# A windowed attention and gated-expert kernel: one written instruction order from the first tile's output stage on, for the DMA queue too, and the second batch's roots in folded form

## The chip, the cores and the metric

The program runs on one core of one Trainium2 chip. A core has five engines with queues of their own: TensorE (PE in the profile; its weight loads are PEld), VectorE (DVE), ScalarE (ACT), GpSimd (POOL) and SyncE (SP), which here issues nearly all DMAs. Each engine takes its own instructions strictly in the order of the program and waits on semaphores for the others. The metric is the device time of one execution in microseconds; the time of a kernel is the median of its runs.

## The reference

Inputs: `q`, `k`, `v` of shape (8 batches, 8 heads, 576 positions, 64), and the weights of a gated expert.

```python
scores = scale * (q @ k.T)                      # per batch and head
mask = (rel >= 0) & (rel < 64)                  # causal window of 64 positions
attn = softmax(where(mask, scores, -1e9))
x = (attn @ v) -> (4608 tokens, 512)            # heads side by side
rms = sqrt(mean(x * x, -1) + 1e-6)
xn = x / rms * rms_g
g, val = xn @ w_gate, xn @ w_val                # 512 -> 1536
out = (g * sigmoid(g) * val) @ w_out            # 1536 -> 512, float32
```

## The kernel before, in words

**Tiling.** Attention runs batch by batch and, in a batch, by pairs of heads: 4 pairs a batch, 32 in all, numbered n = 0 to 31. A batch has 576 tokens; the expert works on 9 tiles of 512 tokens, so tile 1 takes its first 64 tokens from batch 0 and the rest from batch 1, and tile 2 starts with the last 128 tokens of batch 1. Values and weights of the expert are kept as a high and a low half-precision part, and each product is three matmuls (`three`, lines 960 to 962). In tile t the stage *in* (`expert_in`, blocks c = 0 to 5, each two columns groups of gate `pg` and value `pv`) makes the gated activation `h`, and the stage *out* (`expert_out`) sums 6 blocks for each of 4 token groups into `po`, which ACT scales into `ot` and SP stores (L1232). From tile 3 on (`FIRST7`) the in stage uses a seven-product form (`expert_in_7`, `product`, L1136) with combined weights.

**Start.** Batch 0 is done at the start. Meanwhile the weights, which arrive as 8-byte numbers, are loaded into staging buffers (`stage`, L202: three buffers of tag `st8`), widened on ACT, PE and DVE (`widen_powers` L215/L216, `widen_rest` L224 to L227) and split into high and low parts (`split`, L238 to L246). `w_out` is scaled by one common power of two, whose small steps (L306 to L321, with the matmul `obound`) come ahead of its split.

**Combined weights.** `prepare(c, step)` makes the seven combinations of block c of the weights and puts them into a scratch tensor in memory, `sevens`: at step 0 twelve copies of plain blocks (L1091), at others sums on DVE (`sums`, L1061, L1096 to L1109), a high part on ACT (L1083), a low part on DVE (L1073) and two stores (L1075). `load_sevens` (L1119) loads them back into `wt` for tile 3 and later. `PREP` spreads these steps: nine over slots 58.5 to 72, the rest over slots 78 to 192.

**Pairs from batch 2 on** (n >= 8). At `visit(n)` PE makes the products of pair n (`sc`, L399) and the weighted values of pair n-2 (`xp`, L534). Then, a fraction of a slot apart, come masks on DVE (L412), exponentials on ACT (L415), 16 moves on POOL (`pm`, L381) and three transposes on DVE (L386, L388), due ahead of visit n+2. The key load of pair n (`load_kv`, L346 to L360; three buffers) is written 7 steps ahead of visit n; its buffer is that of pair n-3, last used by the sum of squares (L614) behind visit n-1.

**What sets the order.** Work is written into the program at *steps* (32 a tile: 24 for the in stage, 8 for the out stage) or *slots* (48 for an in stage of tiles 0 to 2, 42 later, and 24 for an out stage; one slot of the out stage is one call of `chunk_out`, six matmuls). `at_step` and `at_slot` put a part into `plan`, and `tick` writes what is due between matmul groups. What is written is then placed by the framework's planner, which orders each engine's instructions by its own model of their times, so that an instruction can run ahead of others that were written earlier. `in_written_order(start, engines)` takes that freedom away: from instruction `start` on, each instruction of the listed engines is chained to the one written before it on the same engine, without a semaphore. `strict["on"]` goes with it: while it is on, `defer` writes a copy and a subtraction of the activation one or two ticks later (L1028, L1029) instead of at once.

In the kernel before, `ORDERED = (1, 1)`: the written order starts with block 1 of tile 1, for PE, DVE, ACT and POOL; SP stays with the planner throughout.

**The roots.** After attention each batch needs 1/rms for each of its tokens. For batches 0 and 1 (`b < NRB`) `inverse_roots` sums the squares with five matmul groups (`tot`, L756), which put 128 tokens on partitions and five columns side by side; eleven small DVE steps on 128 x 5 (L774, L811) give the inverse root, and `broadcast` (L835) turns it into a row for all partitions. `normalise` then scales `xb` (L865) and makes both parts of `xn` (L869, L871). The events of batch 1 are due at steps 23.5, 24.5 and 27. For later batches `normalise_all` does the same with the *folded* roots: four matmuls sum the squares with 32 equal columns each (`tot`, L796), so that 144 tokens lie along the free axis and the four quarters of the batch on the four groups of 32 partitions; the eleven steps run on 128 x 144, in three parts; `spread` (L818) makes the row, and `scaled` (L900) and `part` (L910 to L913 for tiles below 3) do the rest. The parts are written a fraction of a slot apart.

Of the kernel before, what the change touches and what calls it, by code (L numbers as in the profile page):

```python
# [42 lines left out]
VISITS = (24.5, 29.5, 35, 41, 47.5)  # L43
MOVES = (8.7, 7, 4.5, 4)
FIRST7 = 3
ORDERED = (1, 1)
PREP = ((27.5, 32, 9), (35, 88, 41))
MASK_AT, MASK_BY, WEIGH = 1, 1, 1
MOVE_AT, MOVE_BY, TURN_AT = 11.3, 0.8, -4
NORM_AT, NORM_BY, NORM_GAP = 5, 0.75, 2  # L50
RUSH = 12
GATE, HH_7, HH_8 = 0, 1, 1
ST = 2 * NBLK * P - D
NRB = 2
S1, LK1, LV1, LQ1 = [-2, 1, 3, 6, 10, 12.5, 15, 18], 2.5, 5, 7
LN2_16 = 16 * math.log(2.0)
MASKED = -3.0e38
# [5 lines left out]
def tile_window_attention_moe(  # L63
# [10 lines left out]
    nc = tc.nc  # L74
# [13 lines left out]
    def in_written_order(start, engines):  # L88

        last = {}  # L90
        for k, ins in enumerate(nc.cur_bb.bb.instructions):
            if ins.engine not in engines:
                continue
            if k >= start and ins.engine in last:
                tc.add_manual_dep(ins, last[ins.engine].name, NO_SYNC, reason="written order")
            last[ins.engine] = ins
# [38 lines left out]
    for rows, cols, own in (  # L135
# [7 lines left out]
        part = mask[rows, cols]  # L143
# [287 lines left out]
    def scores_of_pair(n, sc, first):  # L431
# [19 lines left out]
        whole[n] = p, m, st[:, 2, :]  # L451
        by = MASK_BY if n >= RUSH else 0.5
        for i, u in enumerate(order):
# [177 lines left out]
    def attention_events(b, start, pace, tags):  # L631

        load_queries, load_keys, score, to_keys, values, roots, normal, moved, turned, products, drain, norm = attention(b)
        lk, lv, lq, n0, n1 = tags
        events = []
        if b < NRB:
            events = [(n0 - 1, roots), (n0, partial(normal, 0)), (n1, partial(normal, 1))]
        else:
            s0 = slot_at(visit_at(NPAIR * b + 5))
            for k, part in enumerate(normalise_all(b, norm)):  # L640
                at_slot(s0 + NORM_AT + NORM_BY * k + (NORM_GAP if k > 2 else 0), part)
        for hp in range(NPAIR):
            if b >= TB:
                n = NPAIR * b + hp
                i0 = visit_at(n) - half_steps * (b - 1)
                events.append((i0 - 7, partial(load_queries, hp)))
                events.append((i0 - 7, partial(load_keys, hp)))
                s0 = slot_at(visit_at(n))
                for k in range(16):
                    when = MOVE_AT + MOVE_BY * k if n >= RUSH else MOVE_AT - 4.7 + 0.5 * k  # L650
                    at_slot(s0 + when, partial(moved, hp, k // 4, k % 4))
                for k in range(3):
                    at_slot(slot_at(visit_at(n + 2)) + TURN_AT - 2 * (RUSH <= n < 16) + k, partial(turned, hp, k))
                visits[n] = partial(products, hp), partial(values, hp), partial(drain, hp)
                continue
            i0 = start[2 * hp]
            events.append((i0 - lq, partial(load_queries, hp)))
            events.append((i0 - lq, partial(load_keys, hp)))
            for g in range(2):
                i = start[2 * hp + g]  # L660
                events.append((i + lv, partial(values, hp, g)))
                events.append((i + lk, partial(to_keys, hp, g)))
                events.append((i, partial(score, hp, g)))
        return events
# [4 lines left out]
    def slot_at(h):  # L669

        t, r = divmod(h, half_steps)
        per = 4 * NF if t < FIRST7 else 7 * NC
        first = t * (4 * NF + NC * TT // P) - max(0, t - FIRST7) * (4 * NF - 7 * NC)
        return first + (r * per / in_phase if r < in_phase else per + (r - in_phase) * NC / 2)

    def step_at(s):

        t = 0
        while slot_at(half_steps * (t + 1)) <= s:
            t += 1  # L680
        s -= slot_at(half_steps * t)
        per = 4 * NF if t < FIRST7 else 7 * NC
        return half_steps * t + (s * in_phase / per if s < per else in_phase + (s - per) * 2 / NC)

    def at_slot(s, part):
        at_step(step_at(s) + 1e-6, part)
# [7 lines left out]
    def visit_at(n):  # L694

        n -= NPAIR * TB
        return VISITS[n] if n < 4 else VISITS[4] + 8 * (n - 4)
# [175 lines left out]
    def normalise_all(b, norm):  # L873
        return LazyParts(b, norm).parts()
# [93 lines left out]
    strict = {"on": False}  # L968
# [35 lines left out]
    def expert_in(t, c):  # L1004
        xn = xn_tiles[t]
        hs[t, c] = h_tile(t, c)
        for i in range(2):
            f = 2 * c + i
            fs = slice(i * P, (i + 1) * P)
            hh, hl = hs[t, c][:, 0, i, :], hs[t, c][:, 1, i, :]  # L1010
            acc = []
            for w, name in ((wg, "g"), (wv, "v")):
                tick(0.5)
                a = ps_mo.tile([P, TT], F32, tag="mo", name=f"p{name}_{t}_{f}")
                for kt in range(NKD):
                    if kt == 2:
                        tick(0.5)
                    if True:
                        three(a, w[c][:, 0, kt, fs], w[c][:, 1, kt, fs], xn[:, 0, kt, :], xn[:, 1, kt, :],
                              kt == 0, kt == NKD - 1)  # L1020
                acc.append(a)
                if name == "g":
                    th = wk.tile([P, TT], F32, tag="t2k", name=f"th_{t}_{f}", bufs=T2K)
                    nc.scalar.activation(th, a, AF.Tanh, scale=th_scale[:, c : c + 1])
                    nc.vector.scalar_tensor_tensor(th, th, 1.0, a, ALU.add, ALU.mult)
            nc.vector.scalar_tensor_tensor(th, acc[1], 2.0**-41, th, ALU.mult, ALU.mult)  # L1026
            hi_copy = nc.vector.tensor_copy if t < 2 and E('HHE', 'a' * 24)[12 * t + f] == 'v' else nc.scalar.copy
            defer(HH_8, partial(hi_copy, hh, th))  # L1028
            defer(HH_8 + 1, partial((nc.vector if t and c == NC - 1 else nc.gpsimd).tensor_tensor, hl, th, hh, ALU.subtract))  # L1029
# [204 lines left out]
    def expert_out(t):  # L1234
        for k in range(TT // P):
            halves = 2 if t == NT - 1 and k == TT // P - 1 else 1
            for e in range(halves):
                es = slice(e * DM // halves, (e + 1) * DM // halves)
                po = (ps_mo.tile([P, DM], F32, tag="mo", name=f"po_{t}_{k}_{e}") if t < FIRST7 else banks[(0, 2, 5, 1)[(k + e) % 4]])[:, es]
                for c in range(NC):  # L1240
                    if e == 0:
                        tick(Fraction(2, NC))
                    if t >= FIRST7 and c == k == 0:
                        continue
                    chunk_out(po, t, c, k, c == 0, c == NC - 1, es)
                store(po, t, k, es)
# [17 lines left out]
    def at_step(h, part):  # L1264
        plan.append((h, len(plan), part))
# [3 lines left out]
    for h, part in attention_events(1, S1, 0, (LK1, LV1, LQ1, 24.5, 27)):  # L1269
        at_step(h, part)  # L1270
# [49 lines left out]
    for a, z, count in PREP:  # L1320
        s0, s1 = slot_at(a), slot_at(z)
# [13 lines left out]
    rest(1)  # L1335
    first_full = 1
    for e in SEQ:
        if e[0] == "o":
            expert_out(int(e[1]))
        else:  # L1340
            expert_in(int(e[0]), int(e[1]))
        if e != "o0" and e != "O0" and e[0] != "0":
            first_full = 2
    for t in range(first_full, NTR):
        if t == FIRST7:
            early.close()
            ps_7 = ctx.enter_context(tc.tile_pool(name="ps_7", bufs=1, space=PSUM))
            banks.update((i, ps_7.tile([P, TT], F32, name=f"bk{i}")) for i in (0, 1, 2, 5))
            late = ctx.enter_context(tc.tile_pool(name="late", bufs=1))
            snaps.update((i, late.tile([P, TT], F32, name=i)) for i in ("s1", "u2"))  # L1350
        if t >= FIRST7:
            expert_in_7(t)
        else:
            for c in range(NC):
                strict["on"] |= (t, c) >= ORDERED
                if (t, c) == ORDERED:
                    written = len(nc.cur_bb.bb.instructions)
                expert_in(t, c)
                if t == FIRST7 - 1 and c % 2:
                    load_sevens(c // 2)  # L1360
        expert_out(t)
    assert not plan
    in_written_order(written, [e.engine for e in (nc.tensor, nc.vector, nc.scalar, nc.gpsimd)])
    early.close()


# [35 lines left out]
```

## Time and profile before

| | |
|---|---|
| median of 3 runs | 1026.49 us (1024.73 to 1028.15) |
| profiled execution, its own time | 1029.22 us |
| its span, first to last instruction | 1027.4 us |
| mean granted TensorE clock | 0.981 |
| busy: PE / DVE / ACT / POOL | 971.2 / 646.3 / 508.0 / 508.8 us |
| first output-stage matmul (L960, `po`) | 185.4 us |
| first matmul of tile 1 (`pg`) | 229.6 us |
| copies of plain weight blocks (L1091) | 72, issued from 49.3 to 166.7 us |

How to read it: times are microseconds from the first instruction. A row of the timeline gives start, duration, engine, line, operation, output<-input, and the number of merged instructions (x); in brackets stands the idle time before it and what ended that. In a row of the waits stand the waiter, what it waited for, the sum in us, the number of waits and the longest. A matmul lasts 0.38 us from start to end, but the next one starts 0.22 us after it (0.43 at half clock). SPq rows are issues of DMAs by SP's queue.

### The profile page before, as it was taken

What the parts mean: (1) busy time and instruction counts of PE and PEld (TensorE: products, weight loads), DVE (VectorE), ACT (ScalarE), POOL (GpSimd) and SP (SyncE); (2) the same over time, 40 slices, a digit from 0 to 9 for tenths busy, and PEclk for the clock granted to TensorE, in tenths of its full rate; (3) what the DMA queues carried; (4) which work ended last, traced back from release to release, by engine and by line L of the source; (5) the groups of instructions that cost most, each with busy time, mean ns of one, the idle gap of its engine ahead of it and who ended that gap; (6) DMA issues with size and microseconds to landing.
All of it is one profiled execution on the core that took longest, in us unless ns stands there. A gap on an engine that the chain in (4) does not pass through costs nothing.

```text
span 1027.4 us, 20830 instructions
## 1 busy us (share of the span) xinstructions
PE 971.2 (95%) x7835; PEld 630.7 (61%) x7835; DVE 646.3 (63%) x1721; ACT 508.0 (49%) x1303; POOL 508.8 (50%) x634
## 2 busy tenths in 40 slices
PE   7788979799999999999999999999999999999998
PEld 5544435344544544478747874787478848856875
DVE  5687846744789676656775677666766655522540
ACT  5557767424544545356545654565355524422540
POOL 3334624753976478637773776377647611200210
PEclk9989989799999999999999999999999999999999
DMA  7646683122332555256725672566245515632401
GB/s 281 193 139 202 197 267 78 58 72 68 90 103 66 150 165 169 67 163 197 223 66 170 201 223 67 158 212 211 66 143 170 175 32 159 196 108 92 145 1 41
DMA packets 81316, 143.43 MB, mean 140 GB/s; under 512 B 25792, under 2 KB 38336, under 8 KB 81216
## 3 DMA queue, kind: packets, MB, share of 16 engines
q1 hardware_dynamic: 80640, 140.93, 45.1%
q8 instruction: 61, 1.00, 0.4%
q10 hardware_dynamic: 576, 1.18, 0.3%
q14 instruction: 39, 0.32, 0.1%
HBM read 121.64 MB, written 20.45 MB: 138 GB/s over the span
## 4 chain that ended last, share of the span: by engine, by line
PE 68%; DVE 17%; ACT 7%; issue 3%; DMA 2%; POOL 2%; SPq 0%; DVEq 0%; ACTq 0%; POOLq 0%
PE bk L1136 18%; PE bk L960 5%; PE bk L961 5%; PE bk L962 5%; PE xp L534 4%; PE sc L399 4%; DVE th L1176 3%; ACT th L1167 3%; PE po L962 3%; PE po L961 3%; PE po L960 3%; DVE th L1177 3%; PE pg L962 3%; PE pg L960 3%; PE pv L960 3%
## 5 line engine op out<-in xcount | busy, mean ns | idle before, releaser
L1136 PEld LDWEIGHTS <-wt 128*128 128x128 f16 x3024 | 294.9, 98 | 53.9 <-issue 17.2
L381 POOL TENSOR_TENSOR pm<-pm,st 32x288 f32<-32x288 f32 (+1 forms) x384 | 276.8, 721 | 92.8 <-DVE st L449 53.3
L1136 PE MATMUL bk<-xn,wt 128*128 128x256 f16 x1728 | 209.2, 272 | 10.9 <-DVE th L1177 5.3
L981 POOL TENSOR_TENSOR h<-th,h 128x512 f16<-128x512 f32 x78 | 92.4, 1185 | 195.9 <-ACT h L981 180.4
L1136 PE MATMUL bk<-wt,wt 128*128 128x256 f16 x1224 | 150.4, 273 | 0.3 <-ACT u L1156 0.3
L960 PE MATMUL bk<-wt,h 128*128 128x512 f16 (+1 forms) x300 | 111.3, 371 | 0.0
L962 PE MATMUL bk<-wt,h 128*128 128x512 f16 (+1 forms) x300 | 111.2, 371 | 0.0
L961 PE MATMUL bk<-wt,h 128*128 128x512 f16 (+1 forms) x300 | 111.2, 371 | 0.0
L415 ACT ACTIVATE pm<-pm,st 128x128 f32<-128x128 f32 (+1 forms) x216 | 83.9, 389 | 41.6 <-DVE st L412 40.9
L1167 ACT ACTIVATE th<-bk,hsc 128x256 f32<-128x256 f32 x108 | 50.9, 471 | 98.4 <-DVE bk L1197 66.0
L981 ACT CAST h<-th 128x512 f16<-128x512 f32 x94 | 57.8, 615 | 50.1 <-DVE th L1026 36.1
L1176 DVE SCALAR_TENSOR_TENSOR th<-th,bk 128x256 f32<-128x256 f32 x108 | 45.2, 418 | 54.6 <-ACT th L1167 54.3
L962 PEld LDWEIGHTS <-h 128*128 128x128 f16 x436 | 43.0, 99 | 49.6 <-issue 1.6
L960 PEld LDWEIGHTS <-h 128*128 128x128 f16 x436 | 43.4, 100 | 48.5 <-issue 4.6
L961 PEld LDWEIGHTS <-h 128*128 128x128 f16 x436 | 43.1, 99 | 46.0 <-issue 2.0
L399 PE MATMUL sc<-kv,q 64*64 64x128 f32 (+1 forms) x1056 | 58.0, 297 | 12.2 <-DMA q<-q 5.0
L1197 DVE TENSOR_TENSOR bk<-bk,s 128x512 f32<-128x512 f32 x36 | 24.9, 692 | 57.3 <-PE bk L1136 57.3
L399 PEld LDWEIGHTS sc<-kv,q 64*64 64x64 f32 x1056 | 43.7, 146 | 22.8 <-issue 12.2
L960 PE MATMUL pv<-xn,wt 128*128 128x512 f16 x144 | 55.4, 385 | 2.1 <-ACT wt L239 2.0
L960 PE MATMUL pg<-xn,wt 128*128 128x512 f16 x144 | 55.4, 384 | 0.2 <-ACT wt L245 0.2
L961 PE MATMUL pv<-xn,wt 128*128 128x512 f16 x144 | 55.4, 384 | 0.0
L961 PE MATMUL pg<-xn,wt 128*128 128x512 f16 x144 | 55.3, 384 | 0.0
(191 smaller groups left out, 1769.3 us busy)
## 6 DMA issues: line engine op xcount, KB each, us to landing
wt<-sevens SPq DMA_DIRECT2D x108, 512.0 KB, 4.2
kv<-kv SPq DMA_DIRECT2D x28, 608.0 KB, 4.6
wt<-sevens SPq DMA_DIRECT2D x36, 256.0 KB, 3.3
q<-q SPq DMA_DIRECT2D x28, 288.0 KB, 3.3
kv<-kv SPq DMA_DIRECT2D x56, 128.0 KB, 4.7
out<-ot SPq DMA_DIRECT2D x27, 256.0 KB, 2.0
st<-w_gate SPq DMA_DIRECT2D x6, 1024.0 KB, 6.5
st<-w_val SPq DMA_DIRECT2D x6, 1024.0 KB, 7.0
```

The source lines that it names most:

```text
L381: nc.gpsimd.tensor_tensor(m[to, :us, fr], p[fr, :us, to], r, ALU.mult)
L399: nc.tensor.matmul(out.rearrange("p (n c) -> p n c", c=D), lhsT=qt[hd, j * D : (j + 1) * D], rhs=halves[hd, :1, :] if j == 0 else halves[h ...
L415: nc.scalar.activation(part, part, AF.Exp, bias=low, scale=-1.0, accum_out=total)
L534: nc.tensor.matmul(xp[hd, c * D : (c + 1) * D], lhsT=vv[j][rows, hd], rhs=w, start=True, stop=True, skip_group_check=True,)
L960: nc.tensor.matmul(acc, lhsT=lh, rhs=rh, start=first, stop=False)
L961: nc.tensor.matmul(acc, lhsT=lh, rhs=rl, start=False, stop=False)
L962: nc.tensor.matmul(acc, lhsT=ll, rhs=rh, start=False, stop=last)
L981: part()
L1136: nc.tensor.matmul(acc[:, i * HT : (i + 1) * HT], lhsT=w[:, i, l, kt, :], rhs=b[:, m, kt, :], start=at_start, stop=kt == 1 and j == 2, ski ...
L1167: nc.scalar.activation(cols, acc[:, :HT], AF.Tanh, scale=th_scale[:, c : c + 1])
L1176: nc.vector.scalar_tensor_tensor(cols, cols, 1.0, acc[:, :HT], ALU.add, ALU.mult)
L1177: nc.vector.scalar_tensor_tensor(cols, acc[:, HT:], 2.0**-41, cols, ALU.mult, ALU.mult)
```

## The change

- `ORDERED` becomes the first tile's output stage. The written order and `strict` start there instead of at block 1 of tile 1. So they now take in the output stage of tile 0 and block 0 of tile 1, whose copy and subtraction of `h` are deferred.
- SP is added to the engines in written order, from the same point to the end of the kernel.
- `NRB` goes from 2 to 1: batch 1 takes the folded roots. Its eleven parts are written from slot 46 + 2 = 48 on (the start of the output stage; 46 is the slot of the batch's last values), 0.8 slots apart, with 2 slots more after the three root parts: roots at 48, 48.8 and 49.6, then the two pieces (tile 1's 448 tokens, tile 2's 128) from 52.4 to 58.

```diff
-ORDERED = (1, 1)
+ORDERED = "o0"
...
+NORM1 = 2, 0.8, 2
...
-NRB = 2
+NRB = 1
...
         else:
             s0 = slot_at(visit_at(NPAIR * b + 5))
+            at = NORM_AT, NORM_BY, NORM_GAP
+            if b == 1:
+                s0, at = slot_at(S1[-1] + LV1), NORM1
             for k, part in enumerate(normalise_all(b, norm)):
-                at_slot(s0 + NORM_AT + NORM_BY * k + (NORM_GAP if k > 2 else 0), part)
+                at_slot(s0 + at[0] + at[1] * k + (at[2] if k > 2 else 0), part)
...
     for e in SEQ:
+        if e == ORDERED:
+            strict["on"] = True
+            written = len(nc.cur_bb.bb.instructions)
         if e[0] == "o":
             expert_out(int(e[1]))
...
             for c in range(NC):
-                strict["on"] |= (t, c) >= ORDERED
-                if (t, c) == ORDERED:
-                    written = len(nc.cur_bb.bb.instructions)
                 expert_in(t, c)
...
-    in_written_order(written, [e.engine for e in (nc.tensor, nc.vector, nc.scalar, nc.gpsimd)])
+    in_written_order(written, [e.engine for e in (nc.tensor, nc.vector, nc.scalar, nc.gpsimd, nc.sync)])
```

Visits 8 and 9, which make the products of the third batch's first two pairs, are due at steps 24.5 and 29.5, slots 49.5 and 64.5: inside the first output stage (slots 48 to 72).

## The prediction

> **What bounds the kernel now.** I read the page first, then the waits of the matmul engine by stretch, then windows over the two stretches that stood out, then the timelines of DVE and of the DMA queue there.
>
> ```profile
> span 1027.4 us, 20830 instructions
> ...
> PE 971.2 (95%) x7835; PEld 630.7 (61%) x7835; DVE 646.3 (63%) x1721; ACT 508.0 (49%) x1303; POOL 508.8 (50%) x634
> ...
> PE   7788979799999999999999999999999999999998
> ...
> PEclk9989989799999999999999999999999999999999
> ```
>
> TensorE bounds the kernel. A slice is 25.7 us: from the tenth on PE shows 9 in every slice but the last, and what can still be won lies in the first nine, up to about 231 us, where the granted clock dips as well. The waits of PE after 229 us, seven rows, first and last:
>
> ```profile
> PE bk L1136 <- DVE th L1177: 5.3, 11, 0.7
> ...
> PE bk L1136 <- ACT u L1156: 0.3, 2, 0.2
> ```
>
> None of the seven names a DMA. So a new order of the DMA queue can hardly win there; it can only lose. The two stretches that do lose (columns: PE, PEld, DVE, ACT, POOL busy, granted clock, DMA share, GB/s):
>
> ```profile
> 139.20:144.60 5.40, 0.06 (x2) 0.14 (x2) 2.21 (x14) 1.29 (x2) 0.00 (x0) 0.84 0.84 238
> 144.60:153.40 8.80, 8.45 (x43) 3.61 (x43) 3.91 (x8) 8.39 (x21) 1.84 (x4) 0.52 0.82 294
> 177.70:229.60 51.90, 44.40 (x247) 22.69 (x247) 34.32 (x89) 20.07 (x52) 34.60 (x41) 0.87 0.21 65
> 184.00:194.40 10.40, 9.16 (x45) 4.68 (x45) 10.32 (x21) 7.73 (x14) 9.82 (x9) 0.52 0.39 113
> 204.50:208.00 3.50, 3.50 (x10) 1.31 (x9) 2.40 (x4) 2.00 (x4) 3.21 (x6) 0.54 0.02 5
> ```
>
> ```profile
> PE pw L224 <- ACT mp L215: 5.3, 1, 5.3
> ...
> PE rb L835 <- DVE rm L811: 4.2, 1, 4.2
> PE sc L399 <- DVE st L412: 1.8, 1, 1.8
> PE sc L399 <- DMA kv<-kv: 1.2, 1, 1.2
> ```
>
> The first wait is in 139 to 145; the other three lie in the first tile's output stage, 177.7 to 229.6. After each, PE runs at half clock for some microseconds.
>
> **Part 1: the DMA queue in written order.** The 72 copies of weight blocks to the scratch tensor (L1091) are written from slot 58.5 on, in the first output stage and later. In the kernel before, the planner lets them run ahead into the start of the kernel. With SP bound, none can go before the output stage. What they hold up now:
>
> ```profile
> 129.50 5.79 SPq L1091 DMA_DIRECT2D sevens<-wt  x6
> 135.39 0.41 SPq L202 DMA_DIRECT2D st<-w_val  x1
> 135.91 5.15 SPq L1091 DMA_DIRECT2D sevens<-wt  x6
> ...
> 131.39 0.68 DVE L227 SCALAR_TENSOR_TENSOR wt<-st,pw 128x512 int32<-128x512 int32 x1
> ...
> 143.31 1.19 ACT L215 ACTIVATE mp<-st,ebias 128x1024 bf16<-128x1024 int8 x1 [4.35 <-DMA st<-w_val]
> ...
> DMA to landing us min/median/max: 5.1/7.0/12.6
> ```
>
> The last load of w_val needs a staging buffer that DVE frees at 131.39 + 0.68 = 132.07. It is issued at 135.39, behind six copies: 3.3 us late. It lands at 143.3, after 7.9 us where these loads have a median of 7.0: 0.9 us more, beside six copies. Together 4.2 us, and PE's 5.3 us wait ends on exactly this load. I take 4.2. Below: zero, if another late load takes its place. Above: 4.2 more, half of the 8.45 us of PE work at clock 0.52; I don't count that, since ACT is busy 8.39 of the same 8.80 us and is what is late next.
>
> Moved to the later place, the copies cost SP time: 5.79 us for six, so some 11.6 us at most for each group of twelve, six groups between slots 58.5 and 164. Queue work of PE behind them is in part 4.
>
> **Part 2: the first output stage in written order.** Before, the planner puts the products, masks and exponentials of pairs 8 and 9 and the first `sums` ahead of the stage, into DVE's queue between the small steps that set w_out's scale:
>
> ```profile
> 178.09 0.16 DVE L171 TENSOR_SCALAR oe<-obound 128x1 int32<-128x1 int32 x1
> ...
> 183.37 0.22 DVE L320 TENSOR_SCALAR hsc<-hsc,os 128x6 f32<-128x6 f32 x1
> ...
> 184.81 3.37 DVE L246 SCALAR_TENSOR_TENSOR wt<-wt,hsc,wt 128x1024 f16<-128x1024 f32 x2
> ...
> 188.11 1.65 PE L399 MATMUL sc<-kv,q 64*64 64x128 f32 x22 [1.24 <-DMA kv<-kv]
> 189.69 0.61 PE L961 MATMUL po<-wt,h 128*128 128x512 f16 x1
> ...
> L245 ACT ACTIVATE wt<-wt,hsc x6: 1132/1141/1150, 183.6 to 193.0; 128x1024 f16<-128x1024 f32 x6
> L246 DVE SCALAR_TENSOR_TENSOR wt<-wt,hsc,wt x6: 1270/1478/1759, 184.8 to 195.2; 128x1024 f16<-128x1024 f32 x6
> ```
>
> From L171 to the end of L320 takes 5.5 us for seven steps of at most 0.22 each, 1.3 us. In written order everything of pairs 8 and 9 stands behind the stage's start, so the seven run through and end near 179.4. Then one high part on ACT (1.14) and one low part on DVE (1.27): 181.8. Call it 182; now the product that needs this low part (L961) starts at 189.69. The six low parts follow each other at 1.27, against 1.29 for the six matmuls that use one, so PE is fed about as fast as it works.
>
> From 182 the stage holds 144 matmuls at 0.215 (the next fence: 229.62 - 229.41), 31.0 us; the products of pairs 8 and 9, which now fall inside, 2 x 0.9 = 1.8; the sums and the spreads of the roots (part 3), 1.5; the rest of the half clock at its start, some 2; a wait for the roots, 1.5 (part 3); and 0.8 for stores and odd ends: 38.6, so it ends at 220.6 and not at 229.6. Gain 9.0. Of pair 10, products that ran ahead go back to tile 1: -0.5, within the odd ends.
>
> **Part 3: the second batch's roots.** Removed: ten column products, and the five-column root steps, which sat behind a transpose that waited for POOL. Added: the folded form, as later batches show it.
>
> ```profile
> 229.41 0.38 PE L962 MATMUL po<-wt,h 128*128 128x512 f16 x1
> 229.62 0.38 PE L960 MATMUL pg<-xn,wt 128*128 128x512 f16 x1
> ...
> 201.01 1.30 DVE L386 STREAM_TRANSPOSE pm<-pm 128x512 f32<-128x512 f32 x2 [3.87 <-POOL pm L381]
> 202.24 0.22 DVE L811 SCALAR_TENSOR_TENSOR rm<-rm 128x5 f32<-128x5 f32 x1
> ...
> 184.11 28.01 POOL L381 TENSOR_TENSOR pm<-pm,st 32x288 f32<-32x288 f32 x32 [5.15 <-DVE st L449]
> ...
> L811 DVE SCALAR_TENSOR_TENSOR ssq<-ssq x36: 301/307/640, 310.4 to 826.8; 128x144 f32<-128x144 f32 x36
> ...
> 308.99 0.38 PE tot L796 x8
> 314.65 0.69 PE rb L818 x6
> 319.22 0.47 PE rb L818 x4
> ```
>
> On PE: 0.38 + 0.69 + 0.47 = 1.5. On DVE: eleven steps of 0.31, 3.4 us. The 4.2 us wait for the roots comes from the transposes of pair 8 standing ahead of the last root steps while POOL moves two pairs in 28 us; in written order those transposes come at slot 74, in the next tile, so this wait goes. What is late next: the first spread is written before the fifth group of matmuls, at about 182 + 2 + 0.9 + 4 x 1.29 = 190. DVE has by then six low parts (7.6), the root steps (3.4) and four masks (some 1.2) from 181 on: 193. So PE may wait up to 3.3 us for the roots, or nothing if the planner puts the steps between the low parts, as it does now. I take 1.5, nearer to nothing since POOL, which now moves pairs beside them, is idle there. POOL's low parts of tile 1 stand ahead of most of pair 8's moves and are due 20 us later.
>
> The clock: a rule in the Trainium skill, page "TensorE: Matmul & The Clock Gate", Part 1, says that PE turns cold after an idle window of some 3.4 us. By it the two short waits that I leave in the stage would cost no clock, and the sum would be 2 us lower. The rows here disagree: the longest wait just before the half clock from 184 on is the 1.8 us one, so I keep the 2 us.
>
> **Part 4: the queue order later on.** Each load of a pair's keys is written a little ahead of the release of its buffer, and all that stands behind it on SP now waits: block stores, weight loads, output stores.
>
> ```profile
> SPq L346 <- POOL ssq L614: 17.9, 4, 6.8
> ...
> 248.01 11.18 SPq L1075 DMA_DIRECT2D sevens<-hl  x4
> ```
>
> SP waits so already, four times and 17.9 us between 229 and 445, and its block stores take 11.2 us for four, without a row of PE on it. The weight loads of the later tiles have about two blocks of products to land. Ends: nothing, and the 17.9 us if every such wait came through to PE. I take a loss of 1 us, near nothing. The deferred copies in tile 1's first block have the next products as cover: nothing.
>
> **Sum.** 4.2 + 9.0 - 1.0 = 12.2 us. The profiled execution took 1029.22 us (span 1027.4), 2.7 over the median of 1026.49; 1029.2 - 12.2 = 1017.0, and against the median 1014.3.
>
> **Rivals.** (a) The start gains nothing: another wait (ACT, 95% busy right behind it) takes the place, or the planner leaves the copies where they are. Only the stage gains: 1018.5. For it: ACT's 8.39 of 8.80. Against: SP's binding chains each instruction to the one before. (b) PE waits for the roots in full, 3.3 us, and runs cold once more (1.7): the stage gains 5.5, 1018. (c) More: the half clock at 144 to 153 goes too, and the stage waits for nothing: 4.2 + 3.5 more, 1007. (d) Both gains fail, because the planner's order before the stage moves with the queue: 1024 to 1028. (e) Slower: the key load blocks SP. The block stores behind it keep their buffers, of a pool of eight that also serves the gated activations; ACT then waits for a buffer and PE for ACT. Price: the 17.9 us of part 4, so 1031; it turns the sign once more than 13 us of it reach PE. Against it: no row of PE names it today. A rule of the Trainium skill speaks for (e): page "DMA: Bandwidth & Descriptors", "Anatomy of one DMA", says that a wait of a DMA is held by the issuing sequencer, not by the DMA engines. The trace agrees: SP itself shows these waits.
>
> **How the numbers follow.** Forecast 0.50 (1010 to 1018), (a) 0.14, (b) 0.09, (c) 0.07, (d) 0.09, (e) 0.11. A measurement of this kernel tells 0.3%, 3.1 us, from nothing. Faster: forecast, (a), (b), (c), 0.80; same: (d), 0.09; slower: (e), 0.11. The range leaves out (e) and the ends of (c) and (d): 1005 to 1024.5.
>
> **What would show it.** Right: no L1091 before 185 us, the last w_val load landing near 139; L961 of the output stage from about 178 (182 less the 4.2); tile 1's first product near 216; no PE wait on the roots above 2 us; no PE wait named DMA after it. Wrong: the 5 us wait before L224 still there; a wait of PE at L818 of 3 us or more with half clock behind it; PE waits behind th or wt in tiles 1 and 2, with SP held at L346.

## The result, and the profile after

The changed kernel takes 1010.43 us (median of 6 runs, 1008.7 to 1013.6) against 1026.4 us: a ratio of 0.9847, 95% interval 0.9827 to 0.9867. Run once more beside the last experiment it took 1010.49 us, ratio 0.9849 (0.9828 to 0.9869). The profiled execution took 1013.6 us, 3.2 above the median, as that of before stood 2.8 above its own. Line numbers from 52 on are one higher in the changed kernel, those from 640 on four higher (L614 is L615, L811 is L815, L1091 is L1095).

The head of the page, and its PE and PEclk rows:

```profile
span 1011.8 us, 20741 instructions
...
PE 963.3 (95%) x7820; PEld 626.7 (62%) x7831; DVE 646.7 (64%) x1721; ACT 508.0 (50%) x1303; POOL 504.2 (50%) x634
...
PE   7788997999999999999999999999999999999998
...
PEclk9987999999999999999999999999999999999999
```

The dips of the clock in the sixth and eighth slice are gone, and the fourth has a deeper one. The two longest of PE's waits from 135 to 222 us, where before had 5.3, 4.2, 1.8 and 1.2:

```profile
PE tot L800 <- DVE ssq L615: 4.9, 1, 4.9
PE pv L964 <- DVE th L1029: 0.4, 1, 0.4
```

Busy time in four stretches (PE, PEld, DVE, ACT, POOL, granted clock, DMA share, GB/s):

```profile
137.00:143.00 6.00, 5.67 (x31) 2.54 (x31) 3.82 (x17) 4.79 (x6) 0.00 (x0) 1.00 0.64 210
143.00:150.00 7.00, 6.89 (x49) 3.52 (x49) 4.05 (x10) 7.00 (x20) 1.76 (x4) 1.00 0.89 351
167.80:213.10 45.30, 40.17 (x274) 20.32 (x275) 32.43 (x92) 23.02 (x62) 20.50 (x27) 0.92 0.30 84
174.40:181.20 6.80, 5.81 (x51) 2.88 (x52) 6.73 (x11) 3.65 (x4) 0.00 (x0) 0.50 0.02 4
```

To see where the time went I cut each span at two places: where DVE starts its last step on `pv` of tile 0 (the last product of the input stage is done), and where PE starts tile 1's first product. Between them lies the output stage.

| kernel | median us | ratio to before, 95% | start | stage | rest |
|---|---|---|---|---|---|
| before | 1025.76 to 1026.4 | | 176.4 | 53.2 | 797.8 |
| after | 1010.43 | 0.9847 (0.9827 to 0.9867) | 167.8 | 45.3 | 798.7 |
| after, second time | 1010.49 | 0.9849 (0.9828 to 0.9869) | 165.7 | 44.7 | 798.8 |
| queue not bound | 1015.42 | 0.9899 (0.9866 to 0.9932) | 170.6 | 42.7 | 798.7 |
| queue alone | 1012.57 | 0.9867 (0.984 to 0.9895) | 167.8 | 44.4 | 798.5 |
| four engines alone | 1021.41 | 0.9956 (0.9937 to 0.9975) | 171.5 | 48.9 | 799.3 |
| folded roots alone | 1018.3 | 0.9925 (0.9896 to 0.9953) | 171.5 | 45.3 | 799.5 |
| queue and folded roots | 1011.91 | 0.9856 (0.983 to 0.9882) | 169.4 | 40.3 | 799.3 |
| copies later | 1023.1 | 0.9972 (0.9957 to 0.9987) | 171.7 | 52.8 | 798.6 |
| loads later | 1023.3 | 0.9975 (0.9957 to 0.9993) | 173.1 | 50.2 | 798.5 |
| sums later | 1019.29 | 0.9934 (0.9912 to 0.9956) | 173.2 | 44.8 | 798.5 |
| copies, loads, sums later | 1016.3 | 0.9889 (0.9868 to 0.9909) | 171.2 | 44.2 | 799.1 |
| totals later | 1009.15 | 0.9834 (0.9807 to 0.986) | 164.7 | 42.8 | 798.8 |
| totals later, second time | 1008.99 | 0.9827 (0.981 to 0.9845) | 165.6 | 43.0 | 798.8 |

Start, stage and rest are from one profiled execution each. In the two kernels profiled twice the start differs by 2.1 and 0.9 us and the stage by 0.6 and 0.2. Part of the stage's differences is the clock: the granted clock over the stage is 0.87 in before, 0.92 in after, 0.96 with the sums later and 1.00 with the queue and the folded roots. In the profiled pair the start gave 8.6 us, the stage 7.9, and the rest took 0.9 back.

### The profile page after: what moved, and what is told of

It reads as the page before. It is cut to its first block, busy times and chain, and to the rows that moved or that the text cites. A ratio compares the mean times of both kernels' runs of the same rounds, so it can differ in the third digit from the quotient of the medians.

```text
span 1011.8 us, 20741 instructions
## 1 busy us (share of the span) xinstructions
PE 963.3 (95%) x7820; PEld 626.7 (62%) x7831; DVE 646.7 (64%) x1721; ACT 508.0 (50%) x1303; POOL 504.2 (50%) x634
## 3 DMA queue, kind: packets, MB, share of 16 engines
q1 hardware_dynamic: 80640, 140.93, 42.8%
## 4 chain that ended last, share of the span: by engine, by line
PE 69%; DVE 15%; ACT 9%; issue 3%; DMA 3%; POOL 1%; SPq 0%; DVEq 0%; ACTq 0%
PE bk L1140 19%; PE bk L964 5%; PE bk L965 5%; PE bk L966 5%; PE xp L535 4%; PE sc L400 4%; PE po L964 3%; PE po L966 3%; PE po L965 3%; DVE th L1180 3%; ACT th L1171 3%; DVE th L1181 3%; PE pg L966 3%; PE pv L964 2%; PE pg L965 2%
## 5 line engine op out<-in xcount | busy, mean ns | idle before, releaser
L382 POOL TENSOR_TENSOR pm<-pm,st 32x288 f32<-32x288 f32 (+1 forms) x384 | 273.2, 712 | 91.2 <-DVE st L450 47.7
L966 PEld LDWEIGHTS <-h 128*128 128x128 f16 x436 | 42.8, 98 | 49.4 <-issue 0.8
L965 PEld LDWEIGHTS <-h 128*128 128x128 f16 x436 | 42.8, 98 | 44.7 <-issue 0.3
L964 PE MATMUL pg<-xn,wt 128*128 128x512 f16 x144 | 55.4, 385 | 0.0
L965 PE MATMUL pg<-xn,wt 128*128 128x512 f16 x144 | 55.1, 383 | 0.1
L966 PE MATMUL pg<-xn,wt 128*128 128x512 f16 x144 | 54.8, 383 | 0.4 <-DVE wt L247 0.3
```

The source lines that it names most:

```text
L382: nc.gpsimd.tensor_tensor(m[to, :us, fr], p[fr, :us, to], r, ALU.mult)
L964: nc.tensor.matmul(acc, lhsT=lh, rhs=rh, start=first, stop=False)
L965: nc.tensor.matmul(acc, lhsT=lh, rhs=rl, start=False, stop=False)
L966: nc.tensor.matmul(acc, lhsT=ll, rhs=rh, start=False, stop=last)
```

## The experiments: one part at a time

**The queue not bound.** The changed kernel with one line put back:

```diff
-    in_written_order(written, [..., nc.gpsimd, nc.sync)])
+    in_written_order(written, [..., nc.gpsimd)])
```

> The changed kernel with the DMA queue left to the planner again; the other two parts stay. Theory: the early copies of weight blocks run ahead again and hold up the last w_val load, so PE's wait of about 5 us before the widening matmuls at 139 to 145 us and the half clock behind it come back, 8.6 us in all: about 1019 us; the output stage stays near 45 us from the last value chain to tile 1. Rival: the start got faster because the planner placed the engines' work differently, not because of the queue: then 1010 to 1011 us and no L1095 copy matters.

Measured 1015.42: some 5 us are lost of the 16, between the two forecasts. The copies are back at the start, and the wait at `pw` with them, at 2.6 us. The stage, 42.7, did not suffer.

**The queue alone.** The kernel before, with SP alone in written order from the first output stage on:

```diff
+        if e == "o0":
+            written_sp = len(nc.cur_bb.bb.instructions)
...
+    in_written_order(written_sp, [nc.sync.engine])
```

> The kernel before with the DMA queue alone in written order from the first output stage on. Theory: the whole start gain (5.3 us wait, 4.4 us half clock, less about 1 us slip) and nothing in the output stage, which keeps its 53 us: about 1018 us. Rival (the queue order matters little at the start, or costs later by key loads that block block stores): 1026 us or more, with a wait of PE behind th or wt in tiles 1 and 2.

Measured 1012.57, far more than either forecast: the queue's order alone brings 13.5 us, and in the profiled pair some half of it (8.8 us, beside 8.6 at the start) in the stage, which I had not credited to it at all. PE's waits from 135 to 222:

```profile
PE rb L835 <- DVE xb L865: 2.0, 1, 2.0
PE sc L399 <- DVE st L412: 1.2, 1, 1.2
```

No wait for w_val, and the roots' wait is replaced by a shorter one for a buffer of the second spread.

**The four engines alone,** in written order from the first output stage on, with the old roots and the queue free:

```diff
-NRB = 1
+NRB = 2
-    in_written_order(written, [..., nc.gpsimd, nc.sync)])
+    in_written_order(written, [..., nc.gpsimd)])
```

> The kernel before with the four engines in written order from the first output stage on; roots of the second batch as before, DMA queue with the planner. Theory: pairs 8 and 9 no longer stand in front of the scale steps, and the transposes no longer stand in front of the roots: the stage gains 6 to 8 us, the start nothing: 1018 to 1020 us. Rival: without the folded roots PE waits in written order for the old root steps and the two scaling pieces, 3 us or more: 1022 to 1026 us.

Measured 1021.41, the rival's range, and for the rival's reason. The longest of PE's waits from 135 to 222:

```profile
PE rb L839 <- DVE rm L815: 5.2, 1, 5.2
```

In written order the old column roots are waited for in full, longer than in before (4.2). So this wait takes back a part of what the order brings, and 4.7 us are left.

**The folded roots alone.** The kernel before with `NRB = 1`, `NORM1` and the choice of its slots, the orders as they were.

> The kernel before with the folded roots for the second batch alone. Theory: the planner still puts pairs 8 and 9 ahead, so the stage keeps most of its 53 us; the 4.2 us wait for the roots may shrink: 1022 to 1026 us. Rival: the roots were the whole of the stage's loss (4.2 us wait and 1.7 us of half clock): about 1020 us.

Measured 1018.3, better than both. PE waits for no root in this run (its longest wait in the stage is 1.6 us, at the totals), and the stage takes 45.3 us.

The three parts alone gain 13.5, 4.7 and 7.8 us: 26 in all, where together they gain 16. They remove the same loss in different ways.

## The experiments: what the queue's order does

**The copies later.** The kernel before, and only the copies of L1091 kept on SP behind the output store that is written ahead of them:

```diff
+        if k in marked["store"]:
+            store_seen = ins
+        elif k in marked["copy"] and store_seen is not None:
+            tc.add_manual_dep(ins, store_seen.name, NO_SYNC, ...)
```

> Before, with one thing changed: each of the 72 copies of weight blocks stays behind the output store of tile 0 that is written ahead of it; the rest of the DMA queue and the other engines are free as before. Theory (the copies cost the start alone: 2 to 5 us of waiting for w_val's last load and 3 to 10 us of half clock behind it; the stage's loss has another cause): the last step on pv of tile 0 is at 168 to 171 instead of 176, the output stage still takes 50 to 53 us, total 1018 to 1021. Rival (the copies are all that the queue's order changes): the stage shortens too, to about 45 us, and the time is that of the queue order alone, 1012.6. Rival (what the profiled before lost at the start was an odd execution): the start gains 2 us at most, total 1023 to 1025.

Measured 1023.1, a gain of 2.7 us: the time of the third forecast, though the mechanism is the first's: w_val's last load is issued at 133.79, PE waits 0.2 us at L224, and the clock stays full there. The stage, 52.8, is that of before. PE's three longest waits from 135 to 222:

```profile
PE rb L835 <- DVE rm L811: 4.5, 1, 4.5
PE sc L399 <- DVE st L412: 2.0, 1, 2.0
PE sc L399 <- DMA kv<-kv: 1.5, 1, 1.5
```

**The loads later.** The same with the loads of pairs 10 and 11 in place of the copies.

> Before, with one thing changed: the loads of q, keys and values that are written inside tile 0's output stage (those of pair 10 and the rest of the batch) stay behind the output store written ahead of them; the 72 copies still run ahead. Theory (the stage lost its time to pair 10's products, which came early with their loads, waited 1.2 us for the keys, and stood between the output products): start as before, last step on pv at 172 to 176, but the stage takes 44 to 47 us instead of 53, total 1018 to 1020. Rival (the stage lost its time to the masks and exponentials of pairs 8 and 9 in DVE's queue ahead of w_out's scale, as the prediction said; they are still ahead here): the stage takes 51 us or more, total 1024 to 1026.

Measured 1023.3, between the two forecasts and nearer the rival's. The wait for `kv` is gone, but PE still waits 4.4 us for the roots, and the stage takes 50.2 us.

**The sums later.** In before, five steps of the first weight block's sums run among the small steps of w_out's scale. On DVE:

```profile
179.58 0.76 DVE L1061 TENSOR_TENSOR sum<-wt 128x256 f32<-128x256 f16 x2
...
180.38 0.75 DVE L1061 TENSOR_TENSOR sum<-wt 128x256 f32<-128x256 f16 x2
...
182.10 0.69 DVE L1096 TENSOR_TENSOR sum<-sum,sum 128x512 f32<-128x512 f32 x1
```

They stand there too in the runs of the roots, the copies and the loads alone (174 to 179 us), and in no run with the queue or the four engines bound, where sums come after 188. The edit keeps them on DVE behind w_out's last low part, and touches nothing else:

```diff
+        if k in marked["low"]:
+            low_seen = ins
+        elif k in marked["sum"]:
+            tc.add_manual_dep(ins, low_seen.name, NO_SYNC, ...)
```

> Before, with one thing changed: on DVE the sums of weight blocks stay behind w_out's last low part; the DMA queue and all else are free as before. In before five steps of the first block's sums (179.6 to 183) stand among the small steps that set w_out's scale, and so do they in the runs of the folded roots alone, the copies alone and the loads alone; in every run with the queue or the engines in written order they come after 188. Theory (these early sums are what the stage lost: they delay the scale by 3 us, by that the root steps, and these then fall behind the transposes that wait for POOL): start as before (last step on pv at 173 to 176), from the scale's first step to its last 2.5 us instead of 5.3, root steps done ahead of the transposes, the wait at the spread 2 us or less instead of 4.2, stage 44 to 47 us, total 1016 to 1020. Rival (the sums cost their own 2 to 3 us and no more; the roots still end behind the transposes): stage 50 us, total 1022.5 to 1024.

Measured 1019.29, in the theory's range, by an edit that touches neither the queue nor the roots. DVE in this run:

```profile
174.93 0.16 DVE L171 TENSOR_SCALAR oe<-obound 128x1 int32<-128x1 int32 x1
...
176.87 0.23 DVE L320 TENSOR_SCALAR hsc<-hsc,os 128x6 f32<-128x6 f32 x1
...
191.61 3.21 DVE L1061 TENSOR_TENSOR sum<-wt 128x256 f32<-128x256 f16 x4
194.74 0.57 DVE L811 SCALAR_TENSOR_TENSOR rm<-rm 128x5 f32<-128x5 f32 x1
...
199.11 1.30 DVE L386 STREAM_TRANSPOSE pm<-pm 128x512 f32<-128x512 f32 x2 [3.20 <-POOL pm L381]
```

From L171 to the end of L320 it takes 2.17 us instead of 5.50, with masks of pairs 8 and 9 still among the steps. The last root step now stands ahead of the transposes that wait for POOL; in before it stood behind them, at 202.61. The sums have moved in front of it instead, so PE still waits 2.7 us for the roots, where the theory had 2 or less; pair 10's products have left the stage by themselves, since the planner plans anew. So the 7 us are not shown to be the sums' alone: the loads later, which moved these products too, brought 2.5. The stage takes 44.8 us, 8.4 less than before; up to 5.1 of that, by an estimate from the granted clocks (0.13 of 53.2 us less 0.04 of 44.8), is half clock that no longer follows the waits.

**Copies, loads and sums together.**

> Before, with three things kept back together: the 72 copies and the loads of pairs 10 and 11 behind the output stores that are written ahead of them, and the sums of weight blocks behind w_out's last low part. Theory (these three are all that the queue's written order does; the two parts on the queue were worth 2.7 and 2.5 us alone because the early sums still held the stage): start as with the copies alone (last step on pv at 168 to 172), stage 44 to 46 us, total 1011.5 to 1014.5, that of the queue order alone (1012.6). Rival (another part of the queue's order is needed, such as the block stores in order): the stage takes 48 us or more, total 1016 or more.

Measured 1016.3, the rival's time, though not at the rival's place: the stage takes 44.2 us, as with the whole queue bound (44.4). The 3.7 us that are missing lie ahead of it, 171.2 instead of 167.8; 3.4 us of half clock near 142, after a 0.7 us wait at `pw`, are in this run and not in that one. PE's two longest waits from 135 to 222:

```profile
PE rb L835 <- DVE rm L811: 1.3, 1, 1.3
PE sc L399 <- DVE st L412: 1.2, 1, 1.2
```

So the three account for the stage. What else of the queue's order helps the start stays open, and so does why the planner writes the sums later once the queue is bound.

**Queue and folded roots,** the four engines left to the planner until tile 1's second block.

> Before with the DMA queue in written order from tile 0's output stage on and the second batch's folded roots, but the planner still free on the four engines until tile 1's second block. Theory (queue order and folded roots do nearly all, each by its own cause; the four engines' order adds nothing of its own): start of the queue order alone, stage 43 to 45 us, total 1010 to 1012.5. Rival (the written order of the four engines is worth what it gained alone or more): 1014 or more, with the root steps or w_out's scale behind other work in the stage. A total below 1009 would say that the four engines' order costs something in the change, the 4.9 us wait ahead of the totals.

Measured 1011.91, in the theory's range; it was not run beside the changed kernel, and the 1.5 us between them are within the intervals. Its stage is the shortest, 40.3 where the theory had 43 to 45, and the only one without any half clock. No gain of the four engines' order can be told once the other two parts are there. The queue and the four engines with the old roots were not run.

## The experiments: the wait that the change brings

In the changed kernel one wait is new, 4.9 us at the totals. DVE around it, then ACT, then PE:

```profile
169.62 0.16 DVE L172 TENSOR_SCALAR oe<-obound 128x1 int32<-128x1 int32 x1 [1.13 <-PE obound L312]
...
170.65 0.23 DVE L321 TENSOR_SCALAR hsc<-hsc,os 128x6 f32<-128x6 f32 x1
...
172.09 2.48 DVE L247 SCALAR_TENSOR_TENSOR wt<-wt,hsc,wt 128x1024 f16<-128x1024 f32 x2 [1.16 <-ACT wt L246]
174.49 0.75 DVE L615 TENSOR_TENSOR ssq<-ssq,kv 128x576 f32<-128x576 f32 x1
```

```profile
170.91 2.19 ACT L246 ACTIVATE wt<-wt,hsc 128x1024 f16<-128x1024 f32 x2
173.01 0.67 ACT L620 ACTIVATE kv<-xb 128x576 f32<-128x576 f32 x1
```

```profile
175.39 0.70 PE L800 MATMUL tot<-ssq,one 128*32 128x144 f32 x8 [4.91 <-DVE ssq L615]
176.03 0.61 PE L964 MATMUL po<-wt,h 128*128 128x512 f16 x1
```

The first high part is done near 172.1 and the first low part near 173.3, so the first output product, which needs the high part alone, could start near 172.1 and the second at 173.3. But the totals are written ahead of it, at the stage's first slot, and their last summand stands behind two high parts on ACT and two low parts on DVE. The edit writes the totals, and all that follows them, two groups of products later:

```diff
-NORM1 = 2, 0.8, 2
+NORM1 = 4, 0.8, 2
```

> After, with the second batch's totals, root steps, spreads and what follows written two groups of output products later (first at slot 50 instead of 48). Theory (the 4.9 us wait for the sum of squares ahead of the totals holds the whole output stage, whose first operands are ready about 2.6 us earlier): no PE wait at the totals, first output product near 173.4 instead of 176.0 and at least one half-clock window of 3.4 us less, the roots still in time; 3 to 4 us faster than after, 1006.5 to 1008, ratio to before 0.981. Rival (the low parts of w_out on DVE, 1.27 us each, and the root steps among them pace the stage): the wait moves to the low parts or to the spread, total 1009.5 to 1011. Rival (roots come too late): a wait of 2 us or more at the spread or at tile 1's first product, 1012 or more.

Measured 1009.15, between the theory and the first rival. The wait at the totals is gone and none takes its place at the roots. As this was not run beside the changed kernel, both were run together:

> The changed kernel as it is, on the same chip as the next run, for a direct comparison. Expected at 1010.4, ratio 0.985, with the 4.9 us wait ahead of the totals.

> The kernel with the totals two groups later once more, beside the changed kernel. Theory (the wait of 4.9 us was worth its length less what the low parts take, some 3 us): 3 us faster than the changed kernel beside it, 1007 to 1008.5. Rival (the first run's 1009.15 is all there is; the half clock of 6.8 us starts the stage here too): 1 to 1.5 us faster, within what can be told from nothing.

Measured 1010.49 (1009.6 to 1013.52) and 1008.99 (1008.06 to 1009.44): 1.5 us faster, the rival's size. It is the fastest kernel here. All four of its runs lie below all four of the other, but the intervals of the two ratios overlap. PE's two longest waits with the later totals, from 135 to 222:

```profile
PE po L964 <- ACT wt L246: 1.6, 1, 1.6
PE po L965 <- DVE wt L247: 0.7, 1, 0.7
```

And the half-clock stretch of each, first the changed kernel's second run, then that of the later totals:

```profile
170.80:177.70 6.90, 4.41 (x36) 2.06 (x40) 6.90 (x9) 5.16 (x6) 0.00 (x0) 0.51 0.00 1
```

```profile
169.70:176.60 6.90, 6.01 (x45) 2.89 (x45) 6.74 (x6) 6.11 (x7) 0.00 (x0) 0.51 0.02 5
```

Of the 4.9 us, 2.4 come back as waits for w_out's parts. The half clock stays as long, and PE now does 6.0 us of work in it where it did 4.4, the rest having been spent waiting: half of the 1.6 more is lost, 0.8. That leaves 1.7 us; tile 1 starts 1.8 us earlier (208.6 against 210.4).

## Why the prediction was right, and which terms were not

**The total** was right: 1010.4 lies in the range of 1005 to 1024.5 and at the edge of the forecast's own 1010 to 1018, 3.9 us below the 1014.3 that I named. In the profiled pair the terms came out as 8.6 + 7.9 - 0.9 = 15.6 us, where I had 4.2 + 9.0 - 1.0: the start was far too small, the stage somewhat too large, and the stage's reasons were only partly those I gave. That the stage came so near is in part luck.

**Part 1, the start: 4.2 predicted, 8.6 in the profiled pair.** The mechanism came as told. SP in the changed kernel, and ACT behind it:

```profile
133.86 0.39 SPq L203 DMA_DIRECT2D st<-w_val  x1
...
189.27 0.37 SPq L1236 DMA_DIRECT2D out<-ot  x1
189.68 6.12 SPq L1095 DMA_DIRECT2D sevens<-wt  x12
```

```profile
139.43 1.22 ACT L216 ACTIVATE mp<-st,ebias 128x1024 bf16<-128x1024 int8 x1 [1.21 <-DMA st<-w_val]
```

No copy goes before the stage, the load lands at 139.4 (139 was named), and PE's 5.3 us wait is gone; its longest wait there is one of 0.4 for DVE. The step that failed is the sentence that put the half clock behind it at nothing because "ACT is what is late next". In the stretch from 143 to 150 ACT is busy 7.00 of 7.00 us, and PE still does 6.89 at a granted clock of 1.00: a full ACT held nobody. With 4.2 more, the upper bound given there, the start is 8.4. The later runs temper this: the profiled before had the longest of these waits. The kernels in which the copies still run ahead wait 2.1 to 3.2 us at the same place and start their stage at 170.6 to 173.2, not 176.4; the changed kernel and that with the later totals start it at 164.7 to 167.8. So the 4.2 was taken from a long wait; the copies moved by themselves gained 2.7 us in the medians. What was missing in the profiled pair is of the size of the half clock that I left out.

**Part 2, the stage: 9.0 predicted, 7.9.** The seven small steps take 1.26 us (1.3 was predicted), and the first low part is ready 4.1 us after the bound's product (4.3). That the first sums and the masks held these steps was in the working, but not which: the sums, with the addition of a square that came in front of L320 beside them, held 3.3 us of the 5.5, and the masks of pairs 8 and 9, which the argument named first, 0.9 (2.17 less 1.26). Nor did it say that the delay pushed the last root steps behind the transposes. And it credited the four engines' written order; the runs show that the queue alone moves the sums as well. What was late next was mis-named: I gave 1.5 us to the roots, which are not waited for, and nothing to the totals, which held PE for 4.9, 2.4 of which w_out's parts would have taken anyway. The half clock at the stage's start, taken at some 2, lasts 6.8 us with 5.8 us of PE work in it, and half of that work, 2.9, is lost.

**Part 3, the folded roots.** "This wait goes" held. In the written order of the four engines it takes the folded form: with the old roots PE waits 5.2 us for them. The queue's order alone, with the old roots, also left no wait for them. The first root steps were between the last low parts, the rest right behind them (177.55 to 183.3 us), and PE did not wait, as the sentence on "nothing" had it.

**Part 4, the later queue: a loss of 1.0 predicted, 0.9 in the profiled pair, and yet not shown.** The rest takes 798.5 us also in the kernels with the loads or the sums later, whose queue is free in the later tiles; the 797.8 of before stands alone. PE's one wait on a transfer after 400 us, which before does not have:

```profile
PE bk L1140 <- DMA wt<-sevens: 0.6, 1, 0.6
```

So rival (e) did not happen: the copies, 6.12 us for the first twelve, and the key loads stayed hidden.

**The rivals.** (a) and (d) fell with the start's gain, (b) with the absent wait for roots. (c) was half right: the half clock at 144 to 153 went, but the stage did wait, and has a half clock of 6.8 us of its own. What the Trainium skill says ("TensorE: Matmul & The Clock Gate", Part 1), that PE turns cold after an idle window of some 3.4 us, stays disputed. In the profiled after the half clock sets in 3.9 us into the 4.9 us wait, which agrees with it; in the second execution it sets in 2.5 us into the same wait, and that of the last section comes behind 2.2 us.

## What to carry to other kernels

When a planner fills in what an order leaves free, an edit's parts are not terms of a sum: three parts that gained 13.5, 4.7 and 7.8 us alone gained 16 together, as the queue and the four engines moved the same five sums, and the folded roots and the queue ended the same wait for the last root step. So find, in the traces, what most of the faster kernels share and the slower ones lack, and move that alone; here an edit of DVE's order, with what the planner moved in answer, gave 7 us. And before a term is put at nothing because another engine is busy, ask whether anyone waits for that engine: a full row of ACT is no wait.

## What the runs showed of the hardware that was not expected

The half clock comes in stretches of 3.4, 6.8, 10.2 or 13.7 us, multiples of 3.4, and the same gap does not always bring one. Every kernel has a gap of PE of 2.2 us near 76 to 78.5, at the same transpose. From there to 92.5 the changed kernel, then before:

```profile
76.30:92.50 16.20, 12.15 (x83) 6.62 (x84) 13.29 (x42) 9.30 (x21) 7.14 (x11) 0.68 0.70 233
```

```profile
76.30:92.50 16.20, 11.37 (x93) 5.79 (x93) 13.53 (x42) 9.68 (x22) 8.51 (x11) 0.89 0.90 275
```

A granted clock of 0.68 against 0.89 cost the changed kernel's profiled execution some 1.7 us: block 4's first product of the input stage starts at 136.69 there and at 134.95 in before. Its order has no part in that, since in its second execution that product starts at 134.54. The Trainium skill ("TensorE: Matmul & The Clock Gate", Part 1) says that the windows run free of the program and that the ramp varies from run to run; the stretches agree. It also has PE turn cold after at least one idle window of some 3.4 us, and here, from 78.8 us on in the changed kernel, the half clock came right behind 2.2 us.

The same six copies took SP 5.79 us to issue in before and 4.98 with the queue not bound, in the same place, and the load behind them was issued 1.1 us earlier, at 134.27, 0.8 of it by this. So an issue time read from one execution can be off by some 15%.
